# Transposing DMAs that read SBUF directly, in a fused recurrent-memory attention and gated MLP kernel

## The chip, the cores and the metric

The kernel runs on one core of one Trainium2 chip. The metric is device time in microseconds for one execution of the whole program. A core has five engines that run their own instruction streams and meet at semaphores: TensorE (PE, with its weight loads shown as PEld), VectorE (DVE), ScalarE (ACT), GpSimd (POOL) and SyncE (SP), which here only issues DMAs. SP and ACT each have a DMA queue; all DMAs share 16 DMA engines.

## The reference

Two blocks of two layers each are applied to x, 2048 rows of 448 numbers. The first layer of a block, A, is attention over segments of 32 rows with 8 memory rows carried from segment to segment; the second, B, is a gated MLP.

```python
def A(x, mem0, Wq, Wk, Wv, Wo):              # 16 heads of 256
    mem = mem0
    for s in range(64):                      # one segment after the other
        h = concat([mem, x[32*s:32*s+32]])   # 40 rows
        q, k, v = h@Wq, h@Wk, h@Wv           # per head
        p = softmax(mask(q @ k.T * scale))
        o = sum_over_heads((p @ v) @ Wo)
        mem = o[:8]                          # the recurrence
        out += o[8:]
def B(x, Wg, Wu, Wd):
    g = x @ Wg
    return (g * (g > 0) * (x @ Wu)) @ Wd
x = x + A(layernorm(x)); x = x + B(layernorm(x))
x = x + A(layernorm(x)); x = x + B(layernorm(x))
```

All tensors are bf16. The memory makes the 64 segments of each A a chain.

## The kernel before, in words

Before the loop the kernel multiplies the weights together: Wq with Wk to `A_sb` and Wv with Wo to `B_sb`, so that in the loop scores are (h A) h and outputs are (p h) B. This takes the first 72 us or so.

The main loop has 68 steps, g = 0 to 67. Step g works on segment g of the first A and on segment g - 4 of the second A at once (`LAG` = 4). These two are the two *chains* (0 and 1). Steps 0 to 3 have chain 0 alone, steps 64 to 67 chain 1 alone; in all others `two` is true. The 16 heads are worked off in two halves, 0 and 1. Every second step (odd g from 3) also carries one `Feed`, the MLP work for 64 rows of each chain. I call these *long steps* (about 26 us) and the others *short steps* (about 17.5 us).

Within a step the order is written out by hand in `step`, and the classes and functions of operations keep it: `InOrder` chains DVE, ACT, SP and POOL in the order of the program text, and `mm` and `tr` do the same for TensorE. PSUM banks are dealt out by `bank`, a small planner that counts TensorE's time. The order of a step:

1. `project(0, ...)`: five banks of `prj` = h A for half 0 (A_sb tiles stationary, h's columns `hT` moving). The bank's results are copied to `TQ` and `TZ` by ACT or DVE.
2. `late(...)`: the previous step's `weigh_x(1)`, the products `y` of probabilities and rows for half 1.
3. `memory_0`: scores of the memory rows of half 0 (`Sm`), and their softmax on DVE and ACT, which ends in `PJ`. Then `project(1, ...)`, with the transpose of those probabilities (`flipped`, PSUM tile `pps`, copied to `PT`) inside its last bank, and `weigh_m(0)` (tiles `ya` and `yb`).
4. The other scores (`Sx`), `project_out(0)` (tile `ox`, products of `Y` and `B_sb`), in long steps the MLP (`ups`, `gps`, `dps`), `weigh_m(1)`, `project_last`, `project_out(1)`.
5. `finish`: the new memory columns go from `ox` into `hT` (`set_mem`), the output columns into `OT`. Then `project_early` for the next step, and `weigh_x(0)`.

A softmax is a row of small functions, numbered: x1[3] adds the mask, x1[4] takes the maximum, x1[5] subtracts it, x1[0] is 4 and 5 together, x1[1] is the exponential on ACT, x1[2] sums, divides and writes `PJ`. `PX[0]` and `PX[1]` are the parts of `PJ` for the segment rows of half 0 and 1, `PM` those for the memory rows.

Transposes are made in two ways. On TensorE: `tr` against `ident`, then a copy out of PSUM. Or by DMA, as a transposing DMA from DRAM: `sent` writes the tile to a DRAM scratch tile, and `dma_start_transpose` on SP's queue reads it back turned. Before the change these are by DMA:

- `hk`, the step's rows (h itself, turned from `hT`), in steps with both chains: written by ACT in `send_columns(g+1)` at the end of the step before (`dh`), read by SP at the step's start. The half tile hk[:, 4, 64:128] is a copy on POOL. In the other eight steps `hk_make` does it on TensorE (`kps`) with two ACT copies.
- `xT`, the MLP's input, in long steps with both chains: `fetch` (ACT writes `dxn`).
- `PT` for both halves in long steps and for half 1 in short steps: `fetched` (SP writes `dj` or `dx`, `read_rest` reads it).
- the layernormed input rows, `ahead` to `dx0` to `hT`; these stay as they are.

And on TensorE: the output rows in every long step (`residual`: four transposes of `OT` to the tile `otp`, which DVE adds to `xa`; then the row statistics, and `norm` writes `xn`), half 0's PT in short steps, and all in one-chain steps.

Of the kernel before, what the change touches and what calls it, by code (L numbers as in the profile page):

```python
# [8 lines left out]
BF = mybir.dt.bfloat16  # L9
# [3 lines left out]
ALU = mybir.AluOpType  # L13
AX = mybir.AxisListType

DM = 448
# [11 lines left out]
LAG = 4  # L28
BLK = 2
TB = BLK * SEG  # L30
NT = 28
HI = 128
HW = 4 * HI
# [8 lines left out]
BANKS = (((0, 6), (6, 6), (24, 4), (12, 6), (18, 6)), ((0, 6), (24, 4), (6, 6), (12, 6), (18, 6)))  # L42
# [21 lines left out]
def build_kernel(ctx, tc, A_x, A_mem0, A_Wq, A_Wk, A_Wv, A_Wo, B_W_gate, B_W_up, B_W_down, out,  # L64
                 ntiles=16, nseg=64):
    nc = tc.nc
    P = nc.NUM_PARTITIONS
# [47 lines left out]
            return call  # L115

    dve, act, sp, pool = InOrder(nc.vector), InOrder(nc.scalar), InOrder(nc.sync), InOrder(nc.gpsimd)

    to_read = []

    def sent(src, tag, eng=sp):

        d = dram.tile([src.shape[0], src.shape[1]], BF, tag=f"d{tag}", name=f"d{tag}")
        eng.dma_start(d[:], src)
        return d

    def read_rest():

        while to_read:
            sp.dma_start_transpose(*to_read.pop(0))  # L130

    now = [0]
    free_at = [0] * 8
# [33 lines left out]
    def tr(out, src, idn):  # L167
        in_order(nc.tensor.transpose(out, src, idn))  # L168
        passed(out, 56)
# [15 lines left out]
    pre = prepare.enter_context(tc.tile_pool(name="pre", bufs=6))  # L185
# [416 lines left out]
    class Feed:  # L602


        def __init__(self, i):
# [4 lines left out]
            self.x = xa[i % 3]  # L610
            self.nx = xp[0]

        def residual(self):
            tp = bank([P, 4, 128], BF, "otp")
            for kd in range(4):
                tr(tp[:, kd, :], OT[:, kd, :], ident[:])
            dve.tensor_tensor(self.x[:], tp[:].rearrange("p k d -> p (k d)")[:, 0:DM], self.x[:], op=ALU.add)
            self.statistics(self.first)

        def residual_of(self, ot):  # L620
# [25 lines left out]
                self.scale = rstd  # L646

        def fetch(self):
            sp.dma_start_transpose(xT[:, :, self.n], sent(self.xn[self.n, :], "xn", act)[:])

        def xposed(self):
            self.tps = transpose_tokens(self.xn)
# [127 lines left out]
    def project(hf, chains, hb, j, banks, pre={}, busy=False, first=None, inside=None, head=0, between=None):  # L780

        n = L * len(chains)
        for i0, k in banks:
            ps = pre[i0] if i0 in pre else bank([P, 512], F32, "prj")
            two = len(chains) == 2

            def copies(eng, rows, T):
                if two:
                    evac(eng, T, ps[rows, 0:k * n].rearrange("p (t g q) -> p t g q", t=k, q=16))
                    return  # L790
                c = chains[0]
                src = ps[rows, 0:k * n].rearrange("p (t w) -> p t w", t=k)
                x, m = (0, SEG) if c == 0 else (MEM, 0)
                evac(eng, T[:, :, 2, MEM * c:MEM * c + MEM], src[:, :, m:m + MEM])
                evac(eng, T[:, :, 3 * c:3 * c + 2, :],
                     src[:, :, x:x + SEG].rearrange("p t (g q) -> p t g q", q=16))

            for i in range(k):
                if inside is not None and i == 4:
                    inside()  # L800
                if i0 not in pre:
                    tile_of(ps, hf, i0 + i, i, chains, hb, j, range(4), True, True)
                elif i >= head or i0 != banks[0][0]:
                    tile_of(ps, hf, i0 + i, i, chains, hb, j, range(3), False, True)
            if i0 in pre:
                let_go(ps)
            if first is not None:
                first()
            if between is not None:
                between()  # L810
            if i0 < 24:
                u0, eo = i0 // 12 * 6, i0 // 6 % 2
                T = TQ[hf][:].rearrange("p g u w -> p g (u w)").rearrange("p g (t e q) -> p t e g q", e=2, q=16)
                T = T[:, u0:u0 + 6, eo]
                copies(act if (i0 != 6 if busy and hf else i0 % 12) else dve, slice(0, P), T)
            else:
                for eng, e in ((act if busy else dve, 0), (act, 1)):
                    copies(eng, FR[e], TZ[hf][FR[e]].rearrange("p g (t e q) -> p t e g q", e=2, q=16)[:, :, e])
            if i0 in (6, 18):
                next_piece()  # L820
# [51 lines left out]

    def fetched(src, tag):
        PT = main.tile([P, src.shape[1] // 2, 128], BF, tag=f"PT{tag}", name="PT")
        to_read.append((PT[:], sent(src[:].rearrange("p b w -> p (b w)"), tag)[:]))
        return PT[:].rearrange("p b q -> p (b q)")

    def active(g):
        return [c for c in (0, 1) if 0 <= g - c * LAG < nseg]

    columns = [None]

    def send_columns(g):

        columns[0] = None
        if len(active(g)) == 2:
            d = dram.tile([HW, HI], BF, tag="dh", name="dh")
            act.dma_start(d[:].rearrange("(i p) q -> p i q", p=P),
                          hTb[g // BLK % 2][:, g % BLK, :].rearrange("p (i q) -> p i q", q=HI))
            columns[0] = d  # L890

    def step(g, ff, pre, late):
        chains = active(g)
# [152 lines left out]
        def finish():  # L1046
            let_go(ox)
            if ms:
                src = ox[:, :, M0:M0 + 16].rearrange("p k (c m) -> p k c m", m=MEM)
                set_mem(g + 1, src[:, :, ms[0]:ms[-1] + 1, :], ms)  # L1050
            send_columns(g + 1)
            o = (g - 1) % BLK * SEG
            for c in xs:
                o2 = o + (TB if c == 0 else 0)
                dve.tensor_copy(OT[:, 0:3, o2:o2 + SEG], ox[:, :, XO[c]:XO[c] + SEG])
# [6 lines left out]

        two = len(chains) == 2
        early = ff is not None and two
        rows = columns[0]
        read_rest()
        if two:
            hk = HK[g % 2]
            sp.dma_start_transpose(hk[:].rearrange("p k n -> p (k n)")[:, 0:DM].unsqueeze(1), rows[0:DM, :])
        project(0, chains, hb, j, BANKS[0][0:1], pre,  # L1070
                between=(lambda: (ff.residual(), ff.norm())) if early else None)
        project(0, chains, hb, j, BANKS[0][1:2], pre)
        if two:
            pool.tensor_copy(hk[:, 4, 64:128], hk[:, 3, 0:64])
        else:
            hk = hk_make()
        if ff is not None and not two:
            ff.residual()
        next_piece()
        project(0, chains, hb, j, BANKS[0][2:3], pre, ff is not None)  # L1080
        if early:
            ff.fetch()
        project(0, chains, hb, j, BANKS[0][3:5], pre, ff is not None)
        if ff is not None:
# [76 lines left out]
        if ff is not None:  # L1161
# [12 lines left out]
            x0[2]()  # L1174
            if two:
                joined = fetched(PJ[0], "j")
                read_rest()
                px0, pm = joined[:, 0:256], joined[:, 256:384]
            far = two and ff.second
            feed(0)  # L1180
# [7 lines left out]
            x1[1]()  # L1188
            ff.products(2)
            x1[2]()  # L1190
            if two:
                px1 = fetched(PX[1], "x1")
                read_rest()
            else:
                px0 = flipped(PX[0], 2, "x0", act)
            if not far:
                weigh_m(1, hk, pm)
            ff.gated(2)
# [10 lines left out]
            project_last()  # L1209
            next_piece()  # L1210
            project_out(1, 0, 12)
            if not two:
                px1 = flipped(PX[1], 2, "x1")
            fed = 20 if two else 18
            project_out(1, 12, fed)
            ff.feed_on()
# [1 line left out]
        else:  # L1218
# [7 lines left out]
            short = two and len(xs) == 1  # L1226
            if two:
                x1[3]()
            if two and not short:
                x1[0]()  # L1230
                x1[1]()
            if not two:
                x0[0]()
                x0[1]()
            late_flip = NT if short else 23
            project_out(0, 0, late_flip)
            pm = flipped(PM[1], 1, "m1") if ms else None
            if short:
                x1[0]()
                x1[1]()  # L1240
            project_out(0, late_flip, NT)
            if two:
                x0[4]()
            weigh_m(1, hk, pm)
            if two:
                x1[2]()
                px1 = fetched(PX[1], "x1")
                read_rest()
                x0[5]()
                x0[1]()  # L1250
                x0[2]()
            else:
                x0[2]()
                x1[3]()
                x1[0]()
                x1[1]()
                x1[2]()
            next_piece()
            project_last()
            flip = 10 if not two else 20 if len(xs) == 2 else 25  # L1260
            project_out(1, 0, flip)
            px0 = flipped(PX[0], 2, "x0", act)
            project_out(1, flip, 25)
            if not two:
                px1 = flipped(PX[1], 2, "x1", act)
            next_piece()
            project_out(1, 25, NT)
            if g % 4 == 2:
# [108 lines left out]
```

## Time and profile before

| | |
|---|---|
| median of 3 runs | 1526.32 us (1525.72 to 1526.88) |
| profiled execution, its own time | 1526.68 us |
| its span | 1524.9 us |
| granted TensorE clock | 1.00 |
| PE busy | 1515.7 us (99%) |
| DVE, ACT, POOL busy | 71%, 47%, 8% |
| DMA queues of SP (q1) and ACT (q10), share of 16 engines | 13.3%, 3.4% |
| a short step and a long one | 17.6 and 26.2 us |

How to read it: a line of a group names the source line, the engine, the operation, out<-in by the program's tiles, the shapes and the count, then busy us and the mean ns of one instruction, then the engine's idle time before them. L160 and L168 are the helpers `mm` and `tr`, L106 is `InOrder`'s, so tiles tell the steps apart. A matmul's duration is from its start to its result; the next one starts long before, so what it costs TensorE is the distance between starts. A line of the timeline gives start and length in us, merged over neighbours of one kind. A DMA's time to landing runs from its issue on the queue to the semaphore that tells of all its data.

### The profile page before, as it was taken

Reading aid. Unit: us, or ns where it says so; the run is one execution under the profiler, and the core shown is the slowest. Engines: PE = TensorE matmul, PEld = TensorE weight load, DVE = VectorE, ACT = ScalarE, POOL = GpSimd, SP = SyncE. Lnnn points to the kernel's source line nnn. Section 1 sums busy time; section 2 is a strip of 40 time slices with the busy share of each in tenths; the row PEclk is TensorE's granted clock in tenths of the full one; section 3 lists DMA queues with packets and bytes.
Section 4 is the critical chain, followed back from the end, with each engine's and each line's share of the span. In section 5 each row is a group of like instructions: output and inputs, shape, how many; then the busy total and the mean of one; then the engine's idle time right before and its main releaser. Section 6 shows DMA issues by size and latency. Waiting matters only on the chain.

```text
span 1524.9 us, 89093 instructions
## 1 busy us (share of the span) xinstructions
PE 1515.7 (99%) x40367; PEld 1406.2 (92%) x40367; DVE 1088.9 (71%) x3621; ACT 721.7 (47%) x1973; POOL 115.8 (8%) x228
## 2 busy tenths in 40 slices
PE   9999999999999999999999999999999999999998
PEld 6688999999999999999999999999999999999997
DVE  7766777777777677777677777777777777777765
ACT  6744444454444444544444445444444444444444
POOL 3301010101010010101001000100101010000000
PEclk9999999999999999999999999999999999999999
DMA  8710111111111111111111111111111111111100
GB/s 255 243 41 25 36 39 48 33 45 35 48 32 41 40 39 42 39 42 39 41 36 40 45 34 45 37 44 30 40 47 35 44 36 43 37 32 37 32 7 10
DMA packets 164236, 72.89 MB, mean 48 GB/s; under 512 B 121928, under 2 KB 162960, under 8 KB 163856
## 3 DMA queue, kind: packets, MB, share of 16 engines
q1 hardware_dynamic: 125792, 51.26, 13.3%
q10 hardware_dynamic: 36976, 12.25, 3.4%
q8 instruction: 316, 5.18, 1.4%
q0 software_dynamic: 1088, 3.68, 0.8%
q14 instruction: 64, 0.52, 0.1%
HBM read 23.18 MB, written 22.41 MB: 30 GB/s over the span
## 4 chain that ended last, share of the span: by engine, by line
PE 99%; DVE 1%; issue 0%; ACT 0%
PE prj L160 33%; PE ox L160 26%; PE gps L160 6%; PE ups L160 6%; PE dps L160 6%; PE o L160 5%; PE y L160 4%; PE Sx L160 3%; PE bps L160 1%; PE Sm L160 1%; PE tpw L168 1%; PE aps L160 1%; PE ya L160 1%; PE yb L160 1%; PE pps L168 1%; PE otp L168 0%
## 5 line engine op out<-in xcount | busy, mean ns | idle before, releaser
L160 PE MATMUL prj<-hT,A_sb 128*128 128x80 bf16 (+3 forms) x15232 | 540.4, 199 | 1.0 <-issue 0.8
L160 PEld LDWEIGHTS <-A_sb 128*128 128x128 bf16 (+1 forms) x15232 | 500.7, 99 | 21.2 <-issue 1.7
L160 PEld LDWEIGHTS <-B_sb 128*128 128x128 bf16 (+1 forms) x15008 | 484.0, 103 | 15.1 <-issue 1.8
L160 PE MATMUL ox<-Y,B_sb 128*128 128x80 bf16 (+2 forms) x11256 | 434.8, 200 | 1.3 <-issue 1.2
L106 ACT CAST TQ<-prj 128x480 bf16<-128x480 f32 (+1 forms) x380 | 184.3, 497 | 95.8 <-PE prj L160 82.3
L106 ACT CAST Y<-y 128x128 bf16<-128x128 f32 (+2 forms) x452 | 150.4, 411 | 78.9 <-PE y L160 71.7
L106 ACT ACTIVATE se<-se 128x160 f32<-128x160 f32 (+2 forms) x270 | 81.5, 302 | 179.3 <-DVE se L106 164.5
L106 DVE CAST Y<-y 128x256 bf16<-128x256 f32 (+2 forms) x316 | 135.5, 478 | 38.7 <-PE y L160 38.1
L160 PEld LDWEIGHTS <-Wg_sb 128*128 128x128 bf16 (+2 forms) x2128 | 124.5, 97 | 9.9 <-issue 2.8
L106 DVE CAST TQ<-prj 128x480 bf16<-128x480 f32 (+1 forms) x228 | 125.8, 572 | 8.6 <-PE prj L160 8.2
L160 PE MATMUL gps<-xT,Wg_sb 128*128 128x128 bf16 (+3 forms) x1904 | 128.8, 216 | 0.1
L106 DVE SCALAR_TENSOR_TENSOR hh<-gps,ut 128x512 bf16<-128x512 f32 (+2 forms) x136 | 80.6, 595 | 58.1 <-PE gps L160 37.5
L160 PEld LDWEIGHTS <-hk 40*128 40x128 bf16 (+1 forms) x1950 | 100.3, 96 | 13.2 <-issue 0.4
L106 DVE CAST Y<-ya 128x256 bf16<-128x256 f32 x134 | 56.9, 424 | 77.3 <-PE ya L160 76.7
L160 PEld LDWEIGHTS <-Wu_sb 128*128 128x128 bf16 (+1 forms) x1904 | 105.7, 97 | 5.6 <-issue 0.2
L160 PE MATMUL ups<-xT,Wu_sb 128*128 128x128 bf16 (+3 forms) x1632 | 107.0, 216 | 0.4 <-DVE xT L106 0.4
L106 ACT CAST TZ<-prj 64x320 bf16<-64x320 f32 (+2 forms) x264 | 96.4, 375 | 18.8 <-DVE TZ L106 16.0
L106 DVE TENSOR_REDUCE ssum<-se 128x4 f32<-128x160 f32 (+2 forms) x270 | 73.3, 271 | 42.5 <-ACT se L106 38.8
L106 ACT CAST ut<-ups 128x512 bf16<-128x512 f32 (+1 forms) x102 | 57.2, 561 | 89.7 <-PE ups L160 89.7
L160 PE MATMUL dps<-Wd_sb,hh 128*128 128x448 bf16 (+1 forms) x504 | 98.2, 342 | 0.7 <-DVE hh L106 0.7
L160 PEld LDWEIGHTS <-TQ 128*128 128x128 bf16 x1938 | 85.7, 96 | 1.5 <-ACT TQ L106 1.0
L160 PE MATMUL y<-PT,hk 40*128 40x256 bf16 (+1 forms) x1280 | 86.3, 248 | 0.0
(141 smaller groups left out, 1680.4 us busy)
## 6 DMA issues: line engine op xcount, KB each, us to landing
dh<-hT ACTq DMA_DIRECT2D x60, 128.0 KB, 2.1
dx<-PJ SPq DMA_DIRECT2D x60, 64.0 KB, 1.6
dxn<-xn ACTq DMA_DIRECT2D x29, 128.0 KB, 2.3
wo<-in_A_Wo_dram POOLq DMA_DIRECT2D x8, 448.0 KB, 5.0
nat<-in_A_Wv_dram SPq DMA_DIRECT2D x8, 384.0 KB, 5.7
dj<-PJ SPq DMA_DIRECT2D x30, 96.0 KB, 1.6
nat<-in_A_Wq_dram SPq DMA_DIRECT2D x6, 384.0 KB, 4.1
nat<-in_A_Wk_dram SPq DMA_DIRECT2D x6, 384.0 KB, 5.0
```

Source lines behind the costliest of these rows:

```text
L106: r = f(*a, **k)
L160: in_order(nc.tensor.matmul(out, lhsT, rhs, **k))
L168: in_order(nc.tensor.transpose(out, src, idn))
```

## The change

Every transposing DMA that went through a DRAM scratch tile (all but that of the input rows) reads the SBUF tile itself; `sent`, `to_read`, `read_rest` and `send_columns` go. Besides:

- `turn_rows` turns `OT` by DMA at the start of long steps with both chains; `residual` adds the result from SBUF, and moves, with `norm`, from behind the first bank of `project(0)` to behind the third. Long steps with one chain keep TensorE (`flip_rows`).
- `turn_columns` makes `hk` in all steps from 2 on, as two transposes on SP (three blocks of 128 columns, and one of 64 partitions) at the step's start, behind `turn_rows`, and the POOL copy.
- In short steps half 0's softmax is finished first (x0 and x1 change places), and its PT comes by DMA (`fetched(PX[0])`), except in steps 0 to 3 (`straight`), where TensorE flips it as before. Half 1's PT comes by DMA in all steps but the last.
- In long steps with both chains the copy of bank 12 of half 0 moves from DVE to ACT.

```diff
+        def turn_rows(self):
+            self.rows = main.tile([P, 4, 128], BF, tag="rows", name="rows")
+            sp.dma_start_transpose(self.rows[:], OT[:].rearrange("p k t -> p (k t)"))
...
         def residual(self):
-            tp = bank([P, 4, 128], BF, "otp")
-            for kd in range(4):
-                tr(tp[:, kd, :], OT[:, kd, :], ident[:])
-            dve.tensor_tensor(self.x[:], tp[:].rearrange("p k d -> p (k d)")[:, 0:DM], self.x[:], op=ALU.add)
+            dve.tensor_tensor(self.x[:], self.rows[:].rearrange("p k d -> p (k d)")[:, 0:DM], self.x[:], op=ALU.add)
             self.statistics(self.first)
...
-            sp.dma_start_transpose(xT[:, :, self.n], sent(self.xn[self.n, :], "xn", act)[:])
+            sp.dma_start_transpose(xT[:, :, self.n], self.xn[self.n, :])
...
-                copies(act if (i0 != 6 if busy and hf else i0 % 12) else dve, slice(0, P), T)
+                copies(act if (i0 != 6 if busy and hf else i0 if busy and two else i0 % 12) else dve, slice(0, P), T)
...
-        to_read.append((PT[:], sent(src[:].rearrange("p b w -> p (b w)"), tag)[:]))
+        sp.dma_start_transpose(PT[:], src[:].rearrange("p b w -> p (b w)"))
...
+    def columns_by_dma(g):
+        return g >= 2 and len(active(g)) > 0
+
+    def turn_columns(g):
+        if columns_by_dma(g):
+            hk = HK[g % 2]
+            src = hTb[g // BLK % 2][:, g % BLK, :]
+            sp.dma_start_transpose(hk[:, 0:3, :], src[:, 0:3 * HI])
+            sp.dma_start_transpose(hk[:, 3:4, 0:64], src[0:64, 3 * HI:HW])
+            pool.tensor_copy(hk[:, 4, 64:128], hk[:, 3, 0:64])
...
+        if early:
+            ff.turn_rows()
+        turn_columns(g)
+        project(0, chains, hb, j, BANKS[0][0:2], pre)
+        hk = HK[g % 2] if columns_by_dma(g) else hk_make()
...
         project(0, chains, hb, j, BANKS[0][2:3], pre, ff is not None)
         if early:
+            ff.residual()
+            ff.norm()
             ff.fetch()
...
             weigh_m(1, hk, pm)
+            x0[2]()
+            straight = g < LAG
+            if not straight:
+                px0 = fetched(PX[0], "x0")
             if two:
-                x1[2]()
-                px1 = fetched(PX[1], "x1")
-                read_rest()
-                x0[5]()
-                x0[1]()
-                x0[2]()
+                x1[5]()
             else:
-                x0[2]()
                 x1[3]()
                 x1[0]()
-                x1[1]()
-                x1[2]()
+            x1[1]()
+            x1[2]()
+            px1 = fetched(PX[1], "x1")
```

More of the change, by code (lines that the diff above doesn't have):

```diff
@@ L117, in build_kernel @@
     dve, act, sp, pool = InOrder(nc.vector), InOrder(nc.scalar), InOrder(nc.sync), InOrder(nc.gpsimd)
[L119 to L130, printed above, removed]
     now = [0]
@@ L611, in __init__, with flip_rows @@
             self.nx = xp[0]
+        def turn_rows(self):
+            self.rows = main.tile([P, 4, 128], BF, tag="rows", name="rows")
+            sp.dma_start_transpose(self.rows[:], OT[:].rearrange("p k t -> p (k t)"))
+        def flip_rows(self):
+            self.rows = bank([P, 4, 128], BF, "otp")
+            for kd in range(4):
+                tr(self.rows[:, kd, :], OT[:, kd, :], ident[:])
         def residual(self):
-            tp = bank([P, 4, 128], BF, "otp")
-            for kd in range(4):
-                tr(tp[:, kd, :], OT[:, kd, :], ident[:])
-            dve.tensor_tensor(self.x[:], tp[:].rearrange("p k d -> p (k d)")[:, 0:DM], self.x[:], op=ALU.add)
+            dve.tensor_tensor(self.x[:], self.rows[:].rearrange("p k d -> p (k d)")[:, 0:DM], self.x[:], op=ALU.add)
             self.statistics(self.first)
@@ L879, in active @@
         return [c for c in (0, 1) if 0 <= g - c * LAG < nseg]
[L881 to L890, printed above, removed]
+    def columns_by_dma(g):
[7 more added lines that the diff above has]
+            pool.tensor_copy(hk[:, 4, 64:128], hk[:, 3, 0:64])
     def step(g, ff, pre, late):
@@ L1050, in finish @@
                 set_mem(g + 1, src[:, :, ms[0]:ms[-1] + 1, :], ms)
-            send_columns(g + 1)
             o = (g - 1) % BLK * SEG
@@ L1064, in step @@
         early = ff is not None and two
-        rows = columns[0]
-        read_rest()
[L1067 to L1076, printed above, removed]
+        if early:
[3 more added lines that the diff above has]
+        hk = HK[g % 2] if columns_by_dma(g) else hk_make()
         if ff is not None and not two:
+            ff.flip_rows()
             ff.residual()
@@ L1176, in step @@
                 joined = fetched(PJ[0], "j")
-                read_rest()
                 px0, pm = joined[:, 0:256], joined[:, 256:384]
@@ L1190, in step @@
             x1[2]()
-            if two:
-                px1 = fetched(PX[1], "x1")
-                read_rest()
-            else:
-                px0 = flipped(PX[0], 2, "x0", act)
+            px1 = fetched(PX[1], "x1")
+            if not two:
+                px0 = fetched(PX[0], "x0")
             if not far:
@@ L1211, in step @@
             project_out(1, 0, 12)
-            if not two:
-                px1 = flipped(PX[1], 2, "x1")
             fed = 20 if two else 18
@@ L1228, in step @@
                 x1[3]()
-            if two and not short:
-                x1[0]()
-                x1[1]()
-            if not two:
+            if not short:
                 x0[0]()
@@ L1238, in step @@
             if short:
-                x1[0]()
-                x1[1]()
+                x0[0]()
+                x0[1]()
             project_out(0, late_flip, NT)
             if two:
-                x0[4]()
+                x1[4]()
             weigh_m(1, hk, pm)
+            x0[2]()
+            straight = g < LAG
+            if not straight:
+                px0 = fetched(PX[0], "x0")
             if two:
-                x1[2]()
-                px1 = fetched(PX[1], "x1")
-                read_rest()
-                x0[5]()
-                x0[1]()
-                x0[2]()
+                x1[5]()
             else:
-                x0[2]()
                 x1[3]()
                 x1[0]()
-                x1[1]()
-                x1[2]()
+            x1[1]()
+            x1[2]()
+            px1 = fetched(PX[1], "x1")
             next_piece()
             project_last()
[L1260 to L1265, printed above, removed]
+            project_out(1, 0, 10)
+            if straight:
+                px0 = flipped(PX[0], 2, "x0", act)
+            project_out(1, 10, 25)
             next_piece()
```

## The prediction

> **What bounds the kernel now.** I read the busy shares and the chain of work first, then TensorE's own waits, its groups by form, the DMA issues with their landings, and last the timeline of one pair of steps from the middle of the run.
>
> ```profile
> PE 1515.7 (99%) x40367; PEld 1406.2 (92%) x40367; DVE 1088.9 (71%) x3621; ACT 721.7 (47%) x1973; POOL 115.8 (8%) x228
> q8 instruction: 316, 5.18, 1.4%
> PE 99%; DVE 1%; issue 0%; ACT 0%
> ```
> ```profile
> PE dps L160 <- DVE hh L106: 0.7, 1, 0.7
> ```
> The chain is TensorE from end to end, and its longest single wait on data is 0.7 us, once, at the tail. So an instruction taken off TensorE is worth its full issue time, and a wait put onto TensorE costs its full length. The change does both; the sum decides.
>
> ```profile
> L168 PE MATMUL pps<-ident,PJ 128*128 128x128 bf16 x197 | 36.0, 221 | 0.0
> L168 PE MATMUL otp<-ident,OT 128*128 128x128 bf16 x132 | 12.8, 220 | 0.0
> L160 PE MATMUL kps<-ident,hT 128*128 128x128 bf16 x24 | 2.6, 217 | 0.0
> ```
> These three groups shrink. Their 220 ns are pipelined latency; the price is read start to start in the timeline. TensorE, VectorE (DVE) and the SP queue, where a short step (no MLP block) ends and a long one (with it) begins at about 717:
>
> ```profile
> 717.41 0.65 PE L160 MATMUL y<-PT,hk 40*128 40x256 bf16 x10
> 718.65 0.39 PE L168 MATMUL otp<-ident,OT 128*128 128x128 bf16 x4
> 718.88 3.10 PE L160 MATMUL prj<-hT,A_sb 128*128 128x80 bf16 x85
> ...
> 725.56 0.22 PE L168 MATMUL pps<-ident,PJ 128*128 128x128 bf16 x1
> ```
> ```profile
> 717.21 0.41 DVE L106 CAST OT<-ox 128x96 bf16<-128x96 f32 x2
> ...
> 719.08 0.39 DVE L106 TENSOR_TENSOR xa<-otp,xa 128x448 bf16<-128x448 bf16 x1 [0.52 <-PE otp L168]
> ...
> 722.27 1.22 DVE L106 CAST Y<-y 128x512 bf16<-128x512 f32 x3
> ...
> 725.05 0.24 DVE L106 TENSOR_TENSOR PJ<-se,rs 128x80 bf16<-128x80 f32 x1
> ```
> ```profile
> 713.87 0.36 SPq L106 DMA_DIRECT2D dx<-PJ  x1
> 715.43 1.18 SPq L106 DMA_TRANSPOSE PT<-dx  x1
> ```
> The DMAs, with median us from issue to landing, and for xT its spread:
>
> ```profile
> xa<-in_A_x_dram SPq DMA_DIRECT2D x32, 56.0 KB, 2.5
> xa<-xp SPq DMA_DIRECT2D x32, 56.0 KB, 1.9
> hk<-dh SPq DMA_TRANSPOSE x60, 3.2
> PT<-dx SPq DMA_TRANSPOSE x60, 2.7
> xT<-dxn SPq DMA_TRANSPOSE x30, 4.1
> ```
> ```profile
> DMA to landing us min/median/max: 2.5/4.1/4.5
> ```
>
> **TensorE work removed.** Counted in the two programs' orders: 120 otp transposes (4 in each of the 30 long steps with both chains), 82 pps (2 in each of 32 short steps, 18 in the steps with one chain), and 24 kps (6 steps). Four otp fill 718.65 to 718.88, so 0.056 us each; the pps and wide kps are issued at the same rate, the six narrow kps at 0.028. That is 120 x 0.056 = 6.8, 82 x 0.057 = 4.7 and 18 x 0.055 + 6 x 0.028 = 1.2: 12.6 us, all on the bound. [...]
>
> **The rows' new wait (30 long steps).** The residual needed only the transposes on TensorE; now OT goes through SP's queue. SP can issue when OT's second copy ends (717.62), and the residual moves behind the third bank. DVE runs in order, and behind the residual stand its statistics and xn (1.70 us from the residual's start to xn's end), two small rstd operations (0.36), the three Y copies and the softmax of the memory scores (3.02 from the first copy's start to the end of PJ), a TQ copy and the PT copy that ya on TensorE needs (0.76 more). In the trace TensorE's pps came 0.27 us after PJ's end, and ya 0.19 after the PT copy; with four otp gone TensorE is there 0.23 us sooner. Going back from ya (726.24 - 0.23, less 0.05 for a semaphore, 0.76, 3.02, 0.36 and 1.70): the residual must start by 720.12, 2.50 after OT's end, and with 0.09 for semaphores the rows must land within **2.41 us** of issue. What comes later stalls TensorE one for one. The TQ copy that moves from DVE to ACT (0.65 us) is what leaves this much; ACT, 47% busy, takes it in its gap before 721.6.
>
> How long is the landing? The same shape from DRAM (xT) took 2.5 at best. Reading SBUF instead of DRAM, the plain copy into xa landed sooner by 0.28 (fastest, 1.82 against 2.10) to 0.56 (medians). So an undisturbed landing of 1.99 to 2.27; I take the middle, 2.13. The nearest rows on either side of all this are 1.5 (fastest plain copy out of SBUF) and 4.5 (slowest xT).
>
> But landings are disturbed. In the trace's DMA packets, 55% of the 240 transposing DMAs land more than 0.2 us behind the fastest of their shape, by 1.26 us in the mean. The cause that stands beside them is the instruction queue q8: single packets of 16 KB, about 1.0 us long, one every 4.76 us in the steady part. Where one starts 0.1 to 2.2 us after the DMA's issue, the landing is late by about 0.15 + 0.8 times that distance, up to 1.9; where it starts later, by nothing. They start when TensorE is near instruction 256k + 214 (quartiles 201 and 233). A pair of steps has 2345 TensorE instructions after the change, 41 more than a multiple of 256, so the long steps walk evenly through the phases. Going through the 30 issues, 10 are hit, by 0.89 in the mean. With a slack of 2.41 - 2.13 = 0.28 that is 10 x 0.61 = **6.1 us** of stalls. At 1.99 it is 4.9, at 2.27 9.0, and at 2.55 (no gain from SBUF) 18.3, since then every step waits.
>
> **Half 0's probabilities in short steps.** x0 takes the place that x1 had: its PJ is ready at 713.84, SP issues at 713.87, and TensorE wants it at 717.41 less 0.11 for the two pps gone, so it may take 3.38 us. The same shape from DRAM needs 2.3 undisturbed and at most 4.4. By the same walk the late ones come within 3.38 in all but a few steps: 0 us if SBUF is quicker, 1.6 if not; I take 0.4. x1 follows at 715.4 and is wanted at 721.8.
>
> **Everything else at nothing, and its cover.** hk is two transposes now, and queued behind the rows; but the write to DRAM ahead of it is gone (2.1 us), which is more than the 1.2 us that SP spends on the rows. POOL's copy (0.24) still follows; TensorE's yb had 0.8 us to spare at the least, 2.9 in the median. If SP were held 2.3 us by a disturbed rows DMA, that least margin would be spent. xT's xn ends some 0.7 us later than 720.87, but the 2.4 us through DRAM go; wanted at 729.05, cover over 2 us. The joined PT and px1 lose 1.6 us of write. In the six one-chain steps kps came 5.0 us ahead of ya and hT's last column is ready before kps, so two DMAs and the copy (up to 5.8 us) nearly always fit; 0.3 us for them and step 66. SP gains 53 issues net, 12 transposes of 1.2 us per 43.8 us pair: not a bound. ACT loses its DRAM sends, kps and PT copies, which bounded nothing. Other instruction packets (8 KB, queue q14) may add 1 us to the rows.
>
> **The sum.** -12.6 + 6.1 + 0.4 + 0.3 + 1.0 = -4.8 us against the profiled execution's own 1526.68 (span 1524.9 and 1.8 around it); the median of the runs lies 0.36 lower. That gives 1521.5; the rows' landing is the soft term, and I forecast **1521**.
>
> **Rivals.**
> - *All hidden.* If SBUF lands near 1.8, the rows' stalls come to 2.4 and the rest to nothing: 1516; at the plain copy's 1.5 about 1514. For it: every plain copy from SBUF lands within 1.9. Against: the transposing ones hold SP 1.15 us before their first packet, whatever the size.
> - *Rows late in every step* (slower). If reading SBUF saves nothing or costs more, DVE's chain behind the residual stalls TensorE in all 30 steps. It decides from 2.41 us; break-even for the whole is near 2.43, where stalls come to the 12.6 saved. At 2.55: -12.6 + 18.3 + 1.6 + 1.3 = +8.6, 1535; at 2.8: 29.8 + 4.3, +22.8, 1549. For it: xT's median is 4.1, and no transpose in the trace landed sooner than 2.26. [...]
> - *No change.* Stalls of 10 to 15 us eat the saving: 1523.5 to 1529.
>
> **Chances.** A measurement of this kernel tells about 0.2% (3 us) from no change. Partly hidden, as forecast, 0.39 (its own range 1517 to 1523); all hidden 0.13; no change 0.13; rows late in every step 0.35. So faster 0.52, same 0.13, slower 0.35. The range leaves out the far end of the slow rival: 1513.5 to 1537.
>
> **What will show it.** otp falls to 12, pps to 115, kps to 8. DMA_TRANSPOSE rows<-OT: a landing median near 2.3 with a tail to 4, fastest near 2.1, bears me out; fastest over 2.4 is the slow rival. TensorE waits appear at pps or ya on DVE's PT or PJ, in about a third of the long steps, in sum 5 to 9 us. I am wrong if SP's hold per SBUF transpose is well over 1.2 us, if y waits for PT in the short steps, or if the waits sit at yb (hk) or ups (xT).

## The result: slower, and what the profile after shows

The changed kernel takes 1538.07 us (median of 6 runs, 1533.31 to 1543.44), the kernel before 1526.60 in the same session (6 runs, 1525.72 to 1527.99). The ratio is 1.0079, 95% interval 1.0057 to 1.0101: about 12 us slower. The changed kernel's runs also scatter more, over 10.1 us against 2.3. The forecast was 1521, with 1513.5 to 1537 as its range. The profiled execution after took 1537.90 us, span 1536.1.

The page of the changed kernel: busy shares, the instruction queue, and the chain that ended last.

```profile
PE 1508.7 (98%) x40141; PEld 1396.5 (91%) x40141; DVE 1066.1 (69%) x3589; ACT 719.3 (47%) x1952; POOL 117.4 (8%) x234
q8 instruction: 314, 5.14, 1.4%
PE 89%; DMA 6%; DVE 4%; issue 1%; ACT 0%; SPq 0%; POOLq 0%; POOL 0%; ACTq 0%
```

The 226 transposes are gone, as the groups by form show (count after the x):

```profile
L155 PE MATMUL pps<-ident,PJ 128*128 128x128 bf16 x115 | 24.6, 221 | 0.0
L155 PE MATMUL otp<-ident,OT 128*128 128x128 bf16 x12 | 1.1, 218 | 0.0
```

But TensorE no longer carries the whole chain: 6% of it is DMA and 4% VectorE. TensorE's own waits (us in total, times, longest) name two that did not exist before:

```profile
PE prj L147 <- DVE Y L106: 13.5, 16, 1.5
PE y L147 <- DMA PT<-PJ: 3.2, 7, 0.7
```

The tile `rows` says what VectorE had been waiting for. This view gives the issues with SP's hold in ns, VectorE's idle time before the residual, and the landing:

```profile
L106 SPq DMA_TRANSPOSE rows<-OT x30: 1188/1190/2284, 151.9 to 1428.1; - x30
  DMA rows<-OT: 36.0, 27
DMA to landing us min/median/max: 2.4/3.1/4.3
```

**One long step that is clean and one that is late.** The timeline of the changed kernel, first a long step without a stall:

```profile
326.43 1.19 SPq L106 DMA_TRANSPOSE rows<-OT  x1
...
328.92 0.39 DVE L106 TENSOR_TENSOR xa<-rows,xa 128x448 bf16<-128x448 bf16 x1 [0.63 <-DMA rows<-OT]
330.37 0.61 PE L147 MATMUL y<-PT,hk 40*128 40x256 bf16 x10
...
330.89 1.20 DVE L106 CAST Y<-y 128x512 bf16<-128x512 f32 x3
331.81 0.67 PE L147 MATMUL prj<-hT,A_sb 128*128 128x80 bf16 x14
```

and one with a late landing (3.92 us):

```profile
722.13 1.19 SPq L106 DMA_TRANSPOSE rows<-OT  x1
...
726.07 0.39 DVE L106 TENSOR_TENSOR xa<-rows,xa 128x448 bf16<-128x448 bf16 x1 [2.07 <-DMA rows<-OT]
726.08 0.61 PE L147 MATMUL y<-PT,hk 40*128 40x256 bf16 x10
...
728.04 1.20 DVE L106 CAST Y<-y 128x512 bf16<-128x512 f32 x3
728.76 0.91 PE L147 MATMUL prj<-hT,A_sb 128*128 128x80 bf16 x21 [1.07 <-DVE Y L106]
```

In the clean step VectorE copies y out 0.52 us after TensorE began it (330.37 to 330.89). In the late one the residual, its statistics and xn stand in front, and the copies begin 1.96 us after (726.08 to 728.04). The next prj needs the PSUM bank that the first copy frees, and TensorE stands: it goes on at 728.76, 0.05 us after that copy's end (728.71). Read over the long steps, the time that TensorE lost at this prj is the landing less 2.67 us: 0.40 at a landing of 3.08, 0.78 at 3.46, 1.24 at 3.92, 1.55 at 4.22. In three steps it is 0.2 to 0.4 us less than that, because there TensorE had already lost time to a late PT and reached the prj later. The lost times of both waits, read start to start in the trace (a little more than the table of waits counts as idle), are:

| steps with both chains, us | before | after |
|---|---|---|
| long step without a stall | 26.17 | 25.94 |
| short step | 17.55 | 17.44 |
| stalls at prj (late rows) | 0 | 16.3 in 17 of 30 long steps |
| stalls at y (late PT of half 0) | 0 | 4.6 in 8 of 30 |
| 29 pairs of steps together | 1265.7 | 1276.8 |

The 29 pairs gain 29 x (0.23 + 0.11) = 9.9 us, and lose 20.3 in the two waits (20.9 less the 0.6 of the 30th pair). That makes 10.4 of the 11.1 us by which they grew.

**What makes a landing late.** DMA packets between issue and landing, changed kernel; first a landing of 2.5 us (326.43 to 328.91), then one of 3.5 (766.83 to 770.29):

```profile
q1 hardware_dynamic: 553, 0.13, 27.0%
```
```profile
q1 hardware_dynamic: 576, 0.13, 27.2%
q8 instruction: 1, 0.02, 2.2%
q14 instruction: 1, 0.01, 1.0%
```

The late one shares its time with packets of the queues that the profile calls instruction (the instruction packets): here the 16 KB one of q8 begins 0.64 us after the issue and takes 1.22 us. The whole execution has 314 of them for 40141 matmuls and as many weight loads, so one for 256 TensorE instructions (80282 / 314; a matmul with its weight load counts as two). The rows are 512 data packets of 256 B. Counting these and the 4 B packets that come behind them, to the nearest tenth of a us after the issue (the left one is the landing of 2.41 issued at 283.05; packets of the next DMA, which begin at 2.5 there, are not counted):

```
                  landing 2.41          landing 3.46
256 B, 1.2-1.7    456, each 15-44 ns    413, each 15-47 ns
256 B, 1.8-1.9     56, each 18 ns        70, five of them 696-841 ns
256 B, 2.0-2.7      0                    29, one to seven per 0.1 us
4 B               1.8 to 2.1            2.9 to 3.1
```

Undisturbed, 80 to 90 packets start every 0.1 us on 16 DMA engines, some five per engine. Behind the instruction packet one to seven start, 29 in all, where one engine's share of the 512 would be 32. From these counts I estimate that one engine's share queues behind the 16 KB packet; the trace names no engine, so this last step is not shown. All 17 rows that land at 2.87 us or later have an instruction packet (q8, or the 8 KB of q14) starting between 0.4 us before and 2.3 us after their issue; of the 13 that land by 2.66 none has one starting between 0 and 2.3.

### The profile page after: what moved, and what is told of

The parts are those of the page before. It is cut to its first block, busy times and chain, and to the rows that moved or that the text cites. A ratio compares the mean times of both kernels' runs of the same rounds, so it can differ in the third digit from the quotient of the medians.

```text
span 1536.1 us, 88689 instructions
## 1 busy us (share of the span) xinstructions
PE 1508.7 (98%) x40141; PEld 1396.5 (91%) x40141; DVE 1066.1 (69%) x3589; ACT 719.3 (47%) x1952; POOL 117.4 (8%) x234
## 4 chain that ended last, share of the span: by engine, by line
PE 89%; DMA 6%; DVE 4%; issue 1%; ACT 0%; SPq 0%; POOLq 0%; POOL 0%; ACTq 0%
PE prj L147 27%; PE ox L147 25%; PE gps L147 6%; PE ups L147 6%; PE dps L147 6%; PE o L147 4%; DMA rows<-OT 4%; PE Sx L147 3%; PE y L147 3%; DMA PT<-PJ 2%; PE bps L147 1%; PE ya L147 1%; PE Sm L147 1%; PE aps L147 1%; PE tpw L155 1%; PE yb L147 1%
## 5 line engine op out<-in xcount | busy, mean ns | idle before, releaser
L147 PE MATMUL prj<-hT,A_sb 128*128 128x80 bf16 (+3 forms) x15232 | 535.4, 199 | 14.2 <-DVE Y L106 13.5
L147 PE MATMUL ox<-Y,B_sb 128*128 128x80 bf16 (+2 forms) x11256 | 430.4, 200 | 2.1 <-issue 2.0
L106 ACT CAST TQ<-prj 128x480 bf16<-128x480 f32 (+2 forms) x410 | 198.4, 502 | 72.8 <-PE prj L147 55.9
L106 DVE CAST TQ<-prj 128x480 bf16<-128x480 f32 (+1 forms) x198 | 109.0, 561 | 16.4 <-PE prj L147 15.9
L106 ACT CAST TZ<-prj 64x320 bf16<-64x320 f32 (+2 forms) x264 | 96.5, 376 | 20.3 <-DVE TZ L106 16.0
```

The source lines that it names most:

```text
L106: r = f(*a, **k)
L147: in_order(nc.tensor.matmul(out, lhsT, rhs, **k))
```

## The experiments

Each ratio is to the kernel before, run on the same chip in the same session. The kernel before took 1528.40 there for the first four kernels, 1526.95 for the next four and 1526.49 for the last three. The expectations of the first four were reckoned from the 1526.60 and 1538.07 of the result, so 1.8 us have to be added to their times. The ratios are not the quotients of the medians given and can differ from them by some hundredths of a per cent.

**1. Rows back on TensorE.** The residual stands behind the first bank, as its rows are there at once.

```diff
-        if early:
-            ff.turn_rows()
         turn_columns(g)
-        project(0, chains, hb, j, BANKS[0][0:2], pre)
+        project(0, chains, hb, j, BANKS[0][0:1], pre, between=rows_first if early else None)
+        project(0, chains, hb, j, BANKS[0][1:2], pre)
...
-            ff.residual()
-            ff.norm()
```

where `rows_first` calls `ff.flip_rows()`, `ff.residual()` and `ff.norm()`.

> Undone alone: the output rows are turned on TensorE again, with the residual behind the first bank as before; all else is the changed kernel. Theory 1 (the loss is TensorE's wait behind the rows' landing, 16.3 us in 17 long steps of the profile after, against 6.8 us of otp saved): 1538.1 - 16.3 + 6.8 = 1528.6, between 1527 and 1530, and the waits of prj for DVE's Y gone; waits of y for PT stay near 4.6 us. Rival (the transposing DMAs that read SBUF, or the new order of half 0 and half 1, cost by themselves, wherever the rows are turned): 1535 or more.

Measured: 1531.02 (1528.00 to 1535.32, 10 runs), ratio 1.0015, 1.0005 to 1.0025. The waits of prj on VectorE's Y are gone; what is left is

```profile
PE y L147 <- DMA PT<-PJ: 4.5, 9, 1.4
```

Taking the rows off the DMA path undoes four fifths of the loss, as expected.

**2. Half 0's probabilities in short steps back on TensorE**, rows by DMA:

```diff
-            straight = g < LAG
+            straight = True
```

> Undone alone: half 0's probabilities in short steps are flipped on TensorE again. Theory 1: the waits of y for PT (4.6 us in 8 long steps' beginnings) go, 64 transposes of 0.056 us come back (3.6): 1538.1 - 4.6 + 3.6 = 1537, within its scatter of the changed kernel. Rival (late PT landings feed the rows' lateness too, being just ahead of them on the same queue): the rows' stalls shrink as well, under 1532.

Measured: 1539.08 (1537.95 to 1543.06, 4 runs), ratio 1.0071, 1.0056 to 1.0086. The short step is 17.55 again, y no longer waits for PT, and the rows' 30 landings exceed 2.67 by 15.7 us in sum. The two pps saved per short step are worth about as much as their new wait costs. The rival is out: the rows stay as late when no PT of half 0 goes ahead of them on the queue.

**3. Both back on TensorE.**

> Both undone: rows and half 0's probabilities on TensorE; left of the change are the DMAs that read SBUF without DRAM scratch, hk by DMA in six more steps, the order of the halves and one copy on ACT. Theory 1: 1538.1 - 20.9 + 10.4 = 1527.6, at most 2 us under the kernel before for the 2.2 us of TensorE work that stays removed: 1524.5 to 1527.6. Rival (reading SBUF is itself the cost): over 1530.

Measured: 1528.61 (1526.31 to 1530.16, 10 runs), ratio 0.9998, 0.9989 to 1.0008; long and short steps 26.17 and 17.55, as before the change. What is left of the change there, the transposing DMAs that read SBUF with no copy to DRAM ahead, neither costs nor gains time: TensorE's table of waits names none of those DMAs, before or here.

**4. Rows on TensorE, and half 0's y products behind the next step's first bank**, so that PT may come 0.7 us later. The rows' transposes and the residual move one bank back with it.

```diff
+        while deferred:
+            deferred.pop()()
+        project(0, chains, hb, j, BANKS[0][1:2], pre)
...
-        weigh_x(0, hk, px0)
+        if ff is None and two and len(nxt) == 2:
+            deferred.append(lambda: weigh_x(0, hk, px0))
+        else:
+            weigh_x(0, hk, px0)
```

> Rows on TensorE, half 0's probabilities by DMA, but the products that read them (weigh_x of half 0 after short steps) move behind the first bank of the next step, 0.65 us later, which makes 4.05 us of room for a landing of at most 4.1 in the profile after. Theory 1: both waits gone and 3.6 us of pps saved: 1526.6 - 3.6 - 1 to 2 = 1521 to 1523, faster than both kernels. Rival: the later products push DVE's and ACT's copies into the residual and the memory softmax, and TensorE waits there: 1526 or more.

Measured: 1531.84 (1530.39 to 1533.43, 10 runs), ratio 1.0023, 1.0013 to 1.0032. That was a miss: y's waits on PT fell to 1.4 us, as expected, but the time did not. Nearly every long step is now 26.41 us, 0.24 longer than experiment 1's 26.17, with the same instructions and no wait in the table. The timeline of TensorE, experiment 1 and then experiment 4, shows where it goes:

```profile
325.60 0.60 PE L147 MATMUL prj<-hT,A_sb 64*128 64x80 bf16 x24
326.04 0.65 PE L147 MATMUL y<-PT,hk 40*128 40x256 bf16 x10
326.62 0.82 PE L147 MATMUL prj<-hT,A_sb 128*128 128x80 bf16 x18
```
```profile
544.21 1.35 PE L147 MATMUL prj<-hT,A_sb 64*128 64x80 bf16 x42
545.50 0.61 PE L147 MATMUL y<-PT,hk 40*128 40x256 bf16 x10
546.04 0.82 PE L147 MATMUL prj<-hT,A_sb 128*128 128x80 bf16 x18
```

The y products work on 40 of the 128 operand rows (the first number of the shape), the 24 early prj on 64, the others on 128. In experiment 1 y stands next to the 64-row prj; in experiment 4 it stands between 128-row ones, and TensorE changes twice more between short and full operands. Start to start a change takes 0.13 us (64 to 128 rows, or 128 to 40) or 0.15 (40 to 128) where a prj otherwise takes 0.036; from 64 rows to 40 it takes 0.03. Read from start to start up to half 1's y, that is 0.16 of the 0.24 us. The other 0.08 is a wait too short for the table: behind half 1's y the second 64-row prj starts 0.086 us after the first, where it was 0.003 in experiment 1, and by the semaphores a copy into TQ released it. That is a small piece of what the rival had foreseen. So a PE order that looks free costs 0.24 us a step, 7 us in all.

**5 and 6. More slack for the rows by TensorE's order.** In the long steps half 1's y products, and VectorE's copies of them, come a bank earlier, ahead of the residual. Experiment 6 also has experiment 2's edit.

```diff
         if early:
+            late(None)
+            late = None
             ff.residual()
```

> The changed kernel with one move in the 30 long steps: the second half's y products, and so VectorE's copies of them, come one bank earlier, ahead of the residual that waits for the rows. Same work, same DMAs. Theory 1 (rows come late because an instruction packet shares the DMA engines, and the lateness costs only what exceeds VectorE's slack): the copies (1.33 us) now run while the rows are on their way, the allowed landing rises from 2.67 to about 4.0 us, and of 17.2 us of excess over 2.67 in the 30 landings of the changed kernel 1.1 are left over 4.0. So some 15 us less than the changed kernel: 3 to 4 us under the kernel before (ratio 0.9975), prj's waits on DVE's Y under 2 us; the waits of y on PT stay near 4. Rival (VectorE is simply too full in this stretch, so the stall moves to the memory scores and to ya): still some 8 to 11 us over the kernel before, with waits at pps or ya.

> The same, and half 0's probabilities in short steps on TensorE again, so that only the rows go by DMA. Theory 1: the 120 otp transposes (6.8 us) are saved and nothing waits for PT: 5 to 7 us under the kernel before (ratio 0.996). Rival: as above, 5 to 11 us over it.

Measured: 1529.95 (1528.32 to 1530.91, 10 runs), ratio 1.0014, 1.0005 to 1.0024; and 1529.82 (1526.99 to 1532.26, 10 runs), ratio 1.0019, 1.0010 to 1.0028. The rows land as late as before (their excess over 2.67 sums to 13.9 and 15.0 us), yet prj's wait on VectorE's Y is gone from both. In experiment 5 one DMA wait is left:

```profile
PE y L147 <- DMA PT<-PJ: 4.4, 9, 1.1
```

So lateness costs only what exceeds the slack: that part is borne out. The time missed its mark by 6 us in the first and some 9 in the second, for 6 of them again through the order: the long step without a stall is 26.15 and not 25.94, as y now stands between two blocks of 128-row prj. Of the 0.23 us of the four otp, 0.21 went into two changes of operand height. The other 3 us of experiment 6 its profile does not show: that execution took 1526.99, the least of its ten, with 29 pairs in 1265.8 us.

**7 and 8. The instruction packets in and out of phase.** In experiment 2's kernel, 22 of the 84 matmuls of half 1's output projection are left out in each long step with both chains, so the output is incomplete. A pair of steps is then 2306 TensorE instructions, 2 more than 9 x 256, and the 16 KB packets (one per 256 instructions) come at nearly the same place in every pair. Experiment 8 differs from 7 only by 77 small matmuls on zeros at the start.

```diff
-            project_out(1, fed, NT)
+            project_out(1, fed, NT, 22 if two else 0)
...
+                    if 0 <= 3 * (t - t0) + mc - 3 < leave:
+                        continue
...
+        for _ in range(77):
+            mm(few[:], still[:, 0:128], still[:, 0:64], start=True, stop=True)
```

> Rows by DMA, half 0's probabilities in short steps on TensorE. Left out: 22 of the 84 matmuls of half 1's output projection in each long step with both chains, so that the output is incomplete. This makes a pair of steps 2306 TensorE instructions, 2 more than 9 times 256, so that the instruction packets come at nearly the same place of every pair; here the rows are issued at TensorE instruction 120 to 180 of 256, where the changed kernel's rows were all late. Theory 1 (the instruction packets make the rows late): all 29 or 30 rows land at 3.5 to 4.3 us and TensorE waits 0.9 to 1.6 at prj in every long step, 35 to 45 us in all. With 23.8 us less of matmuls and rows else as before: 10 to 18 us over the kernel before. Rival (the lateness has to do with the SBUF source, the SP queue or other DMAs, and only falls together with the packets): landings as spread as in the changed kernel, some 16 us of waits, and the same time as its partner.

> The same with the same matmuls left out, and 77 small matmuls on zeros added at the very start (up to 3 us there), which move the rows to TensorE instruction 20 to 80 of 256. Theory 1: all rows land at 2.4 to 2.6 us, prj never waits for DVE's Y; some 29 us under the kernel before (26 if the added matmuls count), 35 to 45 us under its partner. Rival: as its partner within 5 us.

Measured: 1551.56 (1550.92 and 1552.20), ratio 1.0162, 1.0141 to 1.0182, against 1515.70 (1514.83 and 1516.58), ratio 0.9927, 0.9907 to 0.9947. TensorE's waits and the rows' landing, experiment 7:

```profile
PE prj L147 <- DVE Y L106: 37.2, 30, 1.9
PE prj L147 <- DVE hT L106: 8.5, 30, 0.4
```
```profile
DMA to landing us min/median/max: 3.5/4.0/4.7
```

and experiment 8:

```profile
PE prj L147 <- DVE hT L106: 8.5, 30, 0.4
...
PE prj L147 <- DVE Y L106: 0.5, 2, 0.3
```
```profile
DMA to landing us min/median/max: 2.4/2.4/3.1
```

Same work in the loop, 35.9 us apart. The loop alone is further apart, 29 pairs in 1291.0 and 1247.5 us, 43.5 apart, as experiment 8's begins 7.0 us later. The packets fell as meant: in experiment 7 a 16 KB packet starts 0.9 to 2.2 us after the issue of every one of the 30 rows, in experiment 8 none starts between 0.3 before and 2.3 after. In phase, all 30 rows are late; out of phase, three of 30 exceed 2.67 us, by 0.8 in sum. The source in SBUF, SP's queue and the other DMAs are the same in both, so they do not make the rows late; where the instruction packets fall does. Both lie higher than expected, experiment 7 by 7 us or more and experiment 8 by 15 or more: without the 22 matmuls VectorE's copy into hT comes too late in every following short step (8.5 us, in both alike), and the profile of experiment 8 has 2.7 us at tpw, at the start, and a gap of 2.8 at one prj that nothing explains. That spoils the comparison with the kernel before, not the one between the two.

**9 to 11. More slack without touching TensorE's order.** Experiment 9: in the long steps GpSimd (POOL) makes xn and the MLP's scale instead of VectorE. Experiment 10: besides, in short steps ACT copies half 1's memory product ya, so that half 0's probabilities are issued sooner. Experiment 11: experiment 1 (rows on TensorE) with that second edit.

```diff
-            dve.tensor_scalar(out=xn[:, o:o + b - a], in0=t[:, a:b], scalar1=mv[:, 0:1],
+            eng.tensor_scalar(out=xn[:, o:o + b - a], in0=t[:, a:b], scalar1=mv[:, 0:1],
...
+                    pool.tensor_tensor(out=rstd[:], in0=rstd[:], in1=less[:], op=ALU.pow)
...
-            dve.tensor_copy(YB[hf][:, 0:16, M0:M0 + 16], ...)
+            evac(act if hf and ff is None and two else dve, YB[hf][:, 0:16, M0:M0 + 16], ...)
```

> The changed kernel; in the 30 long steps with both chains, xn and the scale move from VectorE to GpSimd (POOL), whose copy into hk stands behind xn now. TensorE's order is untouched, so that no switch between operand heights is added. Theory 1 (a late row costs what exceeds VectorE's slack): VectorE loses 0.9 us behind the residual, the allowed landing goes from 2.67 to about 3.6, and of 17.2 us of excess 4.4 are left; y's waits on PT stay at 4 to 5. So 12 us under the changed kernel, the kernel before within 2 us. Rival: POOL takes 2.5 us for the same xn (its rows of ahead say 1.9 and 0.6), so that ups waits for xT or yb for hk, in all or most steps: still 6 us or more over the kernel before.

> The same, and in short steps ACT instead of VectorE copies the memory product ya of half 1, so that VectorE finishes half 0's probabilities, and SP issues their DMA, about 0.5 us sooner. Theory 1: the allowed landing of half 0's PT goes from 3.4 to 3.9, its waits from 4.6 to under 1 us: 3 to 5 us under the kernel before (ratio 0.997 to 0.998), under both kernels. Rival: ACT's copy comes later than VectorE's and o waits for it in every short step, 0.2 us or more each: no faster than the kernel before.

> Rows on TensorE as in e1_rows_pe, half 0's probabilities by DMA, and ACT's copy of ya as above. Theory 1: e1_rows_pe without its waits of y on PT (4.5 us): 1.5 to 3 us under the kernel before (ratio 0.998 to 0.999). Rival: as above, o waits: 2 us or more over it.

Measured, in this order: 1528.79 (1526.60 to 1533.71, 10 runs), ratio 1.0017, 1.0008 to 1.0026; 1525.65 (1524.97 to 1530.04, 11 runs), ratio 1.0001, 0.9992 to 1.0010; 1524.22 (1522.50 to 1525.46, 10 runs), ratio 0.9982, 0.9973 to 0.9991. The waits of experiment 9:

```profile
PE y L147 <- DMA PT<-PJ: 3.1, 7, 0.6
PE prj L147 <- DVE Y L106: 3.0, 7, 0.6
```

of experiment 10:

```profile
PE prj L147 <- DVE Y L106: 4.9, 9, 1.2
...
PE y L147 <- DMA PT<-PJ: 0.7, 1, 0.7
```

and of experiment 11:

```profile
PE y L147 <- DMA PT<-PJ: 1.1, 1, 1.1
```

In experiment 9 the rows' excess over 2.67 is 17.1 us, as in the changed kernel, and the wait that they cause falls from 13.5 to 3.0: the same late landings, 0.9 us less on VectorE behind them. It ends 2.3 us over the kernel before, where within 2 was expected. The long step without a stall stays 25.94, as TensorE's order is untouched. ACT's copy of ya takes all but one of y's waits away in both kernels that have it. Experiment 10 keeps the whole change and comes level with the kernel before, 2 to 5 us short of what was expected, though its 29 pairs take 1264.3 us against 1265.7. Experiment 11 is faster than both kernels, by 0.18% (2.3 us to the median before): its probabilities go by DMA and its rows stay on TensorE. Its 29 pairs take 1263.7 us.

## Why the prediction was wrong

**The removed work was right in the loop.** The counts of 12 otp and 115 pps are as stated, and 0.23 and 0.11 us per step are the 0.056 x 4 and 0.057 x 2 of the prediction. Of the 12.6 us, 9.9 lie in the steady part and show there. The remaining 2.7, in the first and last steps and the kps, show no gain: outside the steady part the span changed by 0.1 us, and no run shows why.

**The rows' new wait is the term that failed.** It was set at 6.1 us, with 1.0 more for the 8 KB packets, and measured 16.3. That lateness beyond a slack stalls TensorE was right; the place and both factors of the size, how many rows are hit and how hard, were not.
- *The slack held.* An undisturbed landing takes 2.41 to 2.5 us and not 2.13, since reading SBUF saves next to nothing here: the fastest xT lands at 2.3 from SBUF and at 2.5 from DRAM, the fastest PT at 2.26 from either. But the allowed landing is 2.67 and not 2.41. Two errors of the same sign and nearly the same size: that the difference is 0.25, where 0.28 was assumed, is luck.
- *The place was wrong.* TensorE stops not at pps or ya but earlier, at the first prj behind Sm, for the PSUM bank that VectorE's copies of y free. The prediction listed these copies behind the residual and took them for a stretch of VectorE's chain only; that a bank hangs on them was missed.
- *The hits were too few: 17, not 10.* In the profile after, a 16 KB packet that begins 2.31 us after the issue still stands beside the latest landing of all, 4.32 us; one that begins at 2.33 stands beside a landing of 2.50, in time. In the walk through the phases I let a packet count only up to 1.8 us after the issue, and so left out the end of that window (begun at 1.96 in two more steps, it stands beside landings of 4.10 and 3.97). That is at odds with the rule stated just before it, which counts them up to 2.2: walked evenly by that rule, the 30 issues give 12 or 13 hits of 1.03 to 1.07 us and 9 to 10.5 us of stalls, and a forecast of 1524 to 1526. Two more of the 17 are hit by 8 KB packets alone or mainly, which I had put down at 1.0 us by themselves.
- *They were too light.* The 17 landings lie 1.27 us above an undisturbed one in the mean, against 0.89. With a slack of 0.25 that is 17 x 1.0 us = 17, near the 16.3 measured; with the prediction's numbers 10 x 0.61.

**Half 0's probabilities: 0.4 predicted, 4.6 measured.** The allowed time was right (3.40, 3.38 predicted), and so was what happens beyond it. In 7 of 30 steps PT took 3.6 to 4.1 us; the eighth wait, in the first step with both chains, came from a PT issued 1.0 us later than the others. That y waits for PT in short steps was one of the signs named for being wrong. I had said that the late ones come within 3.38 in all but a few steps; a landing of 2.3 plus up to 1.9 of lateness, both of which stood in the prediction, reaches 4.2.

**The rest at nothing was right.** yb does not wait for hk, nor ups for xT beyond the 0.4 us that it waited before, and the DMAs' source is neutral (experiment 3, ratio 0.9998). Nor did xT, of the same shape from DRAM before and from SBUF after, take longer out of SBUF. SP's hold (ns, least, median and most) is about the same:

```profile
L106 SPq DMA_TRANSPOSE xT<-dxn x30: 1200/1202/1862, 157.3 to 1422.4; - x30
```
```profile
L106 SPq DMA_TRANSPOSE xT<-xn x30: 1183/1256/2152, 157.8 to 1433.2; - x30
```

Its fastest landing is 0.2 us sooner from SBUF (2.30 against 2.49); the fastest rows (2.41) land 0.1 later than the fastest xT from the same memory.

**The rivals.** Slower was given 0.35. The time is near what "rows late in every step" gave (1535), and by the letter of its sign it was borne out: a fastest landing over 2.4 was to show it, and the fastest was 2.41, at the very point from which it decides. But rows were not late in every step: 13 of 30 were in time, because the allowed landing was 2.67. It is the forecast's own mechanism with its sizes set too small. No run shows an undisturbed landing of 2.8 us, at which the slow rival's far end, 1549, is reckoned: undisturbed, the rows took 2.41 to 2.5. "All hidden" leaned on plain copies out of SBUF, put at 1.9 at most; in the profile before, the fastest of each kind took 1.53 to 1.95 us and the slowest 2.70 to 4.29, and in the profile after no transposing DMA out of SBUF landed sooner than 2.26. For the rows, transposing on TensorE gives the better kernel here (experiment 1, ratio 1.0015 against 1.0079): four transposes cost TensorE 0.23 us, and the DMA in their place takes 2.4 us undisturbed and up to 4.3. For half 0's probabilities it does not: the best kernel, experiment 11, has them by DMA, with ACT's copy of ya (0.9982), while with both on TensorE (experiment 3) the ratio is 0.9998.

## What to carry to other kernels

Price a new DMA on a tight path by its latest landing and not by its best (here 4.3 us and 2.4), and look for what comes at a fixed period beside it: here the phase between the program's loop and the instruction packets decided how many of the 30 rows came late, all in experiment 7 and three in experiment 8, and the changed kernel, whose loop walks through the phases, lost time to 17. Before moving work off a bounding TensorE, follow every PSUM bank that the engine behind the new wait has to free: the one missed here cost 16.3 us. When the slack has to come from somewhere, take work off the waiting engine (experiment 9: prj's wait from 13.5 us to 3.0); moving TensorE's own instructions can cost as much as it gains, as the changes of operand height did in experiment 5 (0.21 of 0.23 us a step).

## What the runs showed of the hardware that was not expected

- A 16 KB instruction packet, 1.1 us long in the median, one per 256 TensorE instructions, stands beside rows that landed up to 1.9 us later (4.32 against 2.41). Two kernels with the same loop, whose packets fell at different places in it, differed by 35.9 us, 2.4% (43.5 us in the loop itself).
- A change between matmuls on 40 or 64 operand rows and on 128 took TensorE about 0.1 us over the usual 0.036 from start to start. Two more of them a step cost 0.16 us (experiment 4) and 0.21 us (experiment 5). Changes between 64 and 128 operand columns (o to ox, and back) took 0.13 us too.
- Reading SBUF in place of DRAM did not shorten a transposing DMA beyond 0.2 us, though the copy to DRAM ahead of it, 1.6 to 2.3 us in the medians, goes with it.
